# Zero fills between the single transfers of w_up, w_gate and their gradients in the FFN

## Chip, cores, metric

The kernel runs on one core of one Trainium2 chip. The metric is device time in microseconds (us) from launch to end; a kernel's executions agree within about 0.2%. A profiled execution has a span about 2 us shorter than the time that is quoted.

## The reference, cut to what matters

A decode step of one token is run forwards and backwards: adaptive layer norm, attention over the last 4096 positions of a 65536-long cache, a gated FFN. The outputs are the result and the gradients of every input.

```python
def _B_ref(x, w_gate, w_up, w_down):          # D = 1024, F = 3584
    g = jnp.einsum('bsd,df->bsf', x, w_gate)
    u = jnp.einsum('bsd,df->bsf', x, w_up)
    h = _sigmoid(g) * u
    return jnp.einsum('bsf,fd->bsd', h, w_down)
# attention, layer norms, modulation: left out
_out, _vjp = jax.vjp(_f, A_x, A_k_cache, A_v_cache, A_wq, A_wo, B_w_gate, B_w_up, B_w_down, c, w_mod)
```

Two things follow. The gradients of the two caches are zero outside the last 4096 positions, so 120 blocks of some 1 MB must be filled with zeros: 126 of the 186 MB written. They depend on nothing and can be issued at any moment. And with one token the weights are used once, so the kernel moves bytes far more than it computes.

## The kernel before

The FFN goes through F in 14 blocks of 256 columns. Loads of w_up and w_gate and the stores of their gradients are half a megabyte each and use the same three slots in turn; they go through GpSimd's queue, as do the fills. w_down and its gradient go through SyncE's. A row of a w_up block is 256 bf16 values, so its DRAM side is cut in runs of 512 bytes ("short runs" below).

```python
def zero(n, after=None):                 # issue the next n zero fills, 1 MB each
    for _ in range(n):
        if len(zleft) <= keep[0]:        # ten are kept for the end
            return
        ...                              # nc.gpsimd.dma_start(out=region, in_=zeros)

def load_ug(n):
    nc.gpsimd.dma_start(out=ug_slot[n % 3][:, 0, :, :], in_=wu_view[:, :, n * FB:(n + 1) * FB])
    nc.gpsimd.dma_start(out=ug_slot[n % 3][:, 1, :, :], in_=wg_view[:, :, n * FB:(n + 1) * FB])

for n in range(NB):
    ...                                  # gradients of block n into ug (VectorE, ScalarE)
    nc.sync.dma_start(out=wd_dram(out_8, n), in_=wd)        # w_down gradient
    ...                                  # load w_down of block n + 2; front(n + 1)
    nc.gpsimd.dma_start(out=dwu_view[:, :, n * FB:(n + 1) * FB], in_=ug[:, 0, :, :])
    st = nc.gpsimd.dma_start(out=dwg_view[:, :, n * FB:(n + 1) * FB], in_=ug[:, 1, :, :])
    zero(Z_FFN[2 * n])
    if n + 3 < NB:
        load_ug(n + 3)                   # waits until the two stores above have landed
    zero(Z_FFN[2 * n + 1])
```

A GpSimd issue that waits holds up all that stand behind it in the program.

## Time and profile before

| | before |
|---|---|
| time, median | 627.65 us (627.56 to 627.77, 3 runs) |
| bytes moved | 256.42 MB, mean 410 GB/s |
| busiest compute engine | VectorE, 52% of the span |
| rate, FFN (172 to 376 us) | 402 GB/s |
| rate, fills alone (155 to 160 us) | 429 GB/s |

A kernel whose DMA engines are busy in every slice gains only if it moves fewer bytes or moves them faster. So rates by stage are the first thing to read. A bare busy digit does not help: it is 9 in the FFN as well.

### The profile page before, as it was taken

Reading aid. Unit: us, or ns where it says so; the run is one execution under the profiler, and the core shown is the slowest. Engines: PE = TensorE matmul, PEld = TensorE weight load, DVE = VectorE, ACT = ScalarE, POOL = GpSimd, SP = SyncE. Lnnn points to the kernel's source line nnn. Section 1 sums busy time; section 2 is a strip of 40 time slices with the busy share of each in tenths; the row PEclk is TensorE's granted clock in tenths of the full one; section 3 lists DMA queues with packets and bytes.
Section 4 is the critical chain, followed back from the end, with each engine's and each line's share of the span. In section 5 each row is a group of like instructions: output and inputs, shape, how many; then the busy total and the mean of one; then the engine's idle time right before and its main releaser. Section 6 shows DMA issues by size and latency. Waiting matters only on the chain.

```text
span 625.3 us, 8430 instructions
## 1 busy us (share of the span) xinstructions
PE 188.0 (30%) x3324; PEld 164.8 (26%) x3324; DVE 325.4 (52%) x728; ACT 212.8 (34%) x333; POOL 151.4 (24%) x232
## 2 busy tenths in 40 slices
PE   3888176623022121111111113312920013225100
PEld 3877155622021121111111112210720012225000
DVE  3442046203986784746565456999740089930400
ACT  2652157100035342424333234984520013225300
POOL 2000121113223232324323342322311014312320
PEclk9876578655555555555555555555755555555555
DMA  9999999999999999999999999999999999999997
GB/s 353 421 423 418 422 418 420 424 424 423 422 386 389 404 394 407 407 401 409 411 401 407 399 405 417 415 420 426 423 426 424 423 421 429 425 428 426 426 422 263
DMA packets 42647, 256.42 MB, mean 410 GB/s; under 512 B 5149, under 2 KB 5149, under 8 KB 18080
## 3 DMA queue, kind: packets, MB, share of 16 engines
q0 software_dynamic: 31568, 192.95, 80.8%
q1 hardware_dynamic: 10992, 62.93, 29.4%
q8 instruction: 26, 0.43, 0.3%
q14 instruction: 13, 0.11, 0.0%
q10 hardware_dynamic: 48, 0.01, 0.0%
HBM read 70.26 MB, written 185.60 MB: 409 GB/s over the span
## 4 chain that ended last, share of the span: by engine, by line
DMA 65%; DVE 10%; PE 9%; issue 5%; ACT 5%; POOL 3%; ACTq 0%; POOLq 0%; DVEq 0%
DMA out_dram<-arena 34%; DMA out_dram<-zeros 12%; DVE arena L206 7%; DMA arena<-in_B_w_gate_dram 6%; DMA arena<-in_A_k_cache_dram 4%; DMA arena<-in_w_mod_dram 4%; DMA arena<-in_A_wo_dram 4%; PE tp_kv L440 2%; ACT arena L443 1%; POOL arena L539 1%; PE tm_w L349 1%; POOL out_dram L656 1%; ACT arena L824 1%; DMA rows<-in_c_dram 1%; ACT arena L237 1%
## 5 line engine op out<-in xcount | busy, mean ns | idle before, releaser
L171 POOL DMA_DIRECT2D out_dram<-zeros x114 | 64.2, 567 | 187.2 <-DMA out_dram<-zeros 55.2
L237 ACT ACTIVATE arena<-dug_b,h 128x512 bf16<-128x512 bf16 x112 | 71.4, 713 | 13.2 <-DVE dh2acc L206 12.1
L206 DVE CUSTOM_DVE_ANT_0 arena<-arena,dug_b 128x512 bf16<-128x512 bf16 x112 | 69.6, 686 | 0.5
L206 DVE CUSTOM_DVE_ANT_0 arena<-arena 128x1024 bf16<-128x1024 bf16 (+1 forms) x16 | 45.1, 2819 | 43.9 <-DMA arena<-in_w_mod_dram 39.0
L612 PE MATMUL gu_ps<-h_bf,arena 128*128 128x1 bf16 x448 | 16.0, 166 | 128.9 <-issue 97.9
L820 PEld LDWEIGHTS <-arena 8*128 8x128 bf16 x256 | 25.8, 131 | 101.1 <-issue 97.5
L612 PEld LDWEIGHTS <-arena 128*128 128x128 bf16 x448 | 14.1, 105 | 131.0 <-issue 98.4
L206 DVE CUSTOM_DVE_ANT_0 junk<-arena,b1k 128x1024 fp8e4<-128x1024 bf16 x28 | 34.2, 1223 | 15.9 <-DMA arena<-in_B_w_down_dram 15.4
L206 DVE CUSTOM_DVE_ANT_0 arena<-arena,b1k 128x1024 bf16<-128x1024 bf16 x32 | 37.2, 1219 | 0.0
L538 POOL DMA_DIRECT2D arena<-in_B_w_up_dram x14 | 12.8, 915 | 97.7 <-DMA out_dram<-arena 79.1
L824 ACT CAST arena<-ps_kv 128x512 bf16<-128x512 f32 x32 | 16.1, 692 | 57.1 <-DMA out_dram<-arena 57.1
L614 ACT ACTIVATE sg<-gu_ps 128x2 f32<-128x2 f32 x14 | 2.4, 171 | 93.8 <-PE gu_ps L612 93.8
L820 PE MATMUL ps_kv<-DO_hd,arena 8*128 8x128 bf16 x128 | 15.9, 296 | 57.2 <-ACT arena L824 57.2
L237 ACT ACTIVATE arena<-b1k,o_sh 128x1024 bf16<-128x1024 bf16 x24 | 27.2, 1152 | 11.1 <-DVE do_sh L206 11.1
L826 ACT ACTIVATE arena<-ps_kv 128x512 bf16<-128x512 f32 x32 | 16.1, 625 | 37.9 <-DMA out_dram<-arena 37.9
L440 PE MATMUL tp_kv<-ident_bf,arena 128*128 128x128 bf16 x256 | 22.2, 253 | 21.6 <-DMA arena<-in_A_k_cache_dram 13.8
L198 DVE COPY arena<-tp_kv 128x1024 bf16<-128x1024 bf16 x19 | 13.0, 691 | 29.1 <-PE tp_kv L440 29.0
L820 PE MATMUL ps_kv<-Q_hd,arena 8*128 8x128 bf16 x128 | 16.1, 295 | 37.9 <-ACT arena L826 37.9
L349 PEld LDWEIGHTS <-arena 128*128 128x128 bf16 x320 | 25.9, 124 | 0.0
L440 PEld LDWEIGHTS <-arena 128*128 128x128 bf16 x256 | 19.4, 115 | 24.4 <-DMA arena<-in_A_k_cache_dram 14.7
L636 PE MATMUL bc_ps<-ident_bf,dug_bf 128*128 128x128 bf16 x56 | 14.5, 475 | 33.5 <-DVE hh L189 33.5
L443 ACT COPY arena<-tp_kv 128x1024 bf16<-128x1024 bf16 x13 | 13.1, 1011 | 31.8 <-PE tp_kv L440 31.8
(228 smaller groups left out, 491.6 us busy)
## 6 DMA issues: line engine op xcount, KB each, us to landing
out_dram<-zeros POOLq DMA_DIRECT2D x114, 1024.0 KB, 17.2
out_dram<-arena POOLq DMA_DIRECT2D x32, 1024.0 KB, 19.1
out_dram<-arena POOLq DMA_DIRECT2D x36, 512.0 KB, 13.0
arena<-in_A_wq_dram SPq DMA_DIRECT2D x16, 1024.0 KB, 14.4
arena<-in_w_mod_dram SPq DMA_DIRECT2D x8, 1536.0 KB, 20.7
arena<-in_A_wo_dram SPq DMA_DIRECT2D x8, 1024.0 KB, 39.6
arena<-in_B_w_down_dram SPq DMA_DIRECT2D x14, 512.0 KB, 10.5
arena<-in_B_w_up_dram POOLq DMA_DIRECT2D x14, 512.0 KB, 11.5
```

The source lines that it names most:

```text
L171: ins = nc.gpsimd.dma_start(out=region.bitcast(FP32), in_=zeros[:, :])
L198: return nc.vector.tensor_copy(out=out, in_=a)
L206: return nc.vector.tensor_tensor_reduce(out=out, in0=w, in1=b, scale=1.0, scalar=0.0, op0=ALU.mult, op1=ALU.add, accum_out=acc)
L237: return nc.scalar.activation(out=out, in_=b, func=ACT.Copy, scale=col)
L349: nc.tensor.transpose(tp[:, nb * P:(nb + 1) * P], wm_t[j][:, c0:c0 + P], ident_bf[:, :])
L440: nc.tensor.transpose(tp[:, t8 * P:(t8 + 1) * P], src[:, g, t_ * DH:(t_ + 1) * DH], ident_bf[:, :])
L443: last = nc.scalar.copy(out=o, in_=tp[:, :])
L612: nc.tensor.matmul(gu[:, col + jj:col + jj + 1], lhsT=ug[:, k, j, jj::2], rhs=h2_bf[:, j:j + 1], start=(j == 0), stop=(j == KD - 1))
L636: nc.tensor.matmul(ps4[:, k // 2, :, k % 2], lhsT=r["dug_bf"][:, k:k + 1].broadcast_to([P, P]), rhs=ident_bf[:, :], start=(k == 0), stop=( ...
L820: nc.tensor.matmul(ps[:, t4 * DH:(t4 + 1) * DH], lhsT=rows[32 * g:32 * g + HG, t_ * P:(t_ + 1) * P], rhs=hd[32 * g:32 * g + HG, :], start= ...
L824: nc.scalar.copy(out=o, in_=ps[:, :])
L826: nc.scalar.activation(out=o, in_=ps[:, :], func=ACT.Copy, scale=float(scale))
```

## The change

Its intent: no long row of half-megabyte transfers with short runs; a fill stands between them wherever it can. The new lists also have more fills in the FFN (5 + 56 instead of 4 + 50; the later lists then run out earlier).

```diff
-Z_UG = [2, 0, 2]
-Z_FFN = [3, 0, 2, 1, 3, 0, 2, 1, 3, 0, 2, 0, 3, 0, 3, 1, 2, 2, 2, 1, 2, 4, 0, 3, 1, 5, 3, 1]
+Z_UG = [1, 1, 0, 1, 1, 1]
+Z_FFN = [1, 2, 1, 0, ... the same four numbers for each of the 14 blocks ...]
-    def load_ug(n):
-        nc.gpsimd.dma_start(... w_up ...)
-        nc.gpsimd.dma_start(... w_gate ...)
+    def load_ug(n, nz):
+        for k, view in ((0, wu_view), (1, wg_view)):
+            nc.gpsimd.dma_start(out=ug_slot[n % 3][:, k, :, :], in_=view[:, :, n * FB:(n + 1) * FB])
+            zero(nz[k])
     for n in range(3):
-        load_ug(n)
-        zero(Z_UG[n])
+        load_ug(n, Z_UG[2 * n:2 * n + 2])
...
         nc.gpsimd.dma_start(out=dwu_view[...], in_=ug[:, 0, :, :])
-        st = nc.gpsimd.dma_start(out=dwg_view[...], in_=ug[:, 1, :, :])
-        zero(Z_FFN[2 * n])
+        zero(Z_FFN[4 * n])
+        nc.gpsimd.dma_start(out=dwg_view[...], in_=ug[:, 1, :, :])
+        zero(Z_FFN[4 * n + 1])
         if n + 3 < NB:
-            load_ug(n + 3)
-        zero(Z_FFN[2 * n + 1])
+            load_ug(n + 3, Z_FFN[4 * n + 2:4 * n + 4])
+        else:
+            zero(Z_FFN[4 * n + 2] + Z_FFN[4 * n + 3])
```

More of the change, by code (lines that the diff above doesn't have):

```diff
@@ L50 @@
 Z_LN = 2
-Z_UG = [2, 0, 2]
-Z_FFN = [3, 0, 2, 1, 3, 0, 2, 1, 3, 0, 2, 0, 3, 0, 3, 1, 2, 2, 2, 1, 2, 4, 0, 3, 1, 5, 3, 1]
+Z_UG = [1, 1, 0, 1, 1, 1]
+Z_FFN = [1, 2, 1, 0, 1, 2, 1, 0, 1, 2, 1, 0, 1, 2, 1, 0, 1, 2, 1, 0, 1, 2, 1, 0, 1, 2, 1, 0, 1, 2, 1, 0, 1, 2, 1, 0, 1, 2, 1, 0, 1, 2, 1, 0, 1, 2, 1, 0, 1, 2, 1, 0, 1, 2, 1, 0]
 Z_END = [4, 0, 0, 0, 2, 0, 0, 0, 4]
@@ L535, in load_wd @@
         return nc.sync.dma_start(out=wd_slot[n % 2], in_=wd_dram(B_w_down, n))
-    def load_ug(n):
-        nc.gpsimd.dma_start(out=ug_slot[n % 3][:, 0, :, :], in_=wu_view[:, :, n * FB:(n + 1) * FB])
-        nc.gpsimd.dma_start(out=ug_slot[n % 3][:, 1, :, :], in_=wg_view[:, :, n * FB:(n + 1) * FB])
+    def load_ug(n, nz):
+        for k, view in ((0, wu_view), (1, wg_view)):
+            nc.gpsimd.dma_start(out=ug_slot[n % 3][:, k, :, :], in_=view[:, :, n * FB:(n + 1) * FB])
+            zero(nz[k])
     attn_ps = new_acc("attn_ps")
@@ L656 @@
         nc.gpsimd.dma_start(out=dwu_view[:, :, n * FB:(n + 1) * FB], in_=ug[:, 0, :, :])
-        st = nc.gpsimd.dma_start(out=dwg_view[:, :, n * FB:(n + 1) * FB], in_=ug[:, 1, :, :])
-        zero(Z_FFN[2 * n])
+        zero(Z_FFN[4 * n])
+        nc.gpsimd.dma_start(out=dwg_view[:, :, n * FB:(n + 1) * FB], in_=ug[:, 1, :, :])
+        zero(Z_FFN[4 * n + 1])
         if n + 3 < NB:
-            load_ug(n + 3)
-        zero(Z_FFN[2 * n + 1])
+            load_ug(n + 3, Z_FFN[4 * n + 2:4 * n + 4])
+        else:
+            zero(Z_FFN[4 * n + 2] + Z_FFN[4 * n + 3])
     ffn = vt([P, KD], "ffn")
```

## The prediction

> **What bounds the kernel now.** I read the page's slices first, then the stages by windows, then GpSimd's timeline in the FFN (its queue issues every transfer that the change moves), then VectorE's timeline near the end, for slack.
>
> ```profile
> DMA  9999999999999999999999999999999999999997
> GB/s 353 421 423 418 422 418 420 424 424 423 422 386 389 404 394 407 407 401 409 411 401 407 399 405 417 415 420 426 423 426 424 423 421 429 425 428 426 426 422 263
> DMA 65%; DVE 10%; PE 9%; issue 5%; ACT 5%; POOL 3%; ACTq 0%; POOLq 0%; DVEq 0%
> ```
>
> The 16 DMA engines have work in every slice; no compute engine is above 52% of the span. So time is bytes over rate: 256.42 MB at a mean of 410 GB/s. The rate is 420 to 429 nearly everywhere, and 386 to 411 in slices 12 to 24, which are the FFN. Windows of that stage (the last two numbers of a row are DMA share and GB/s):
>
> ```profile
> 155.00:160.00 5.00, 0.00 (x0) 0.00 (x0) 4.86 (x8) 0.00 (x0) 0.53 (x1) 0.50 1.15 429
> 185.00:190.00 5.00, 1.18 (x32) 1.01 (x32) 5.00 (x15) 2.58 (x7) 0.00 (x0) 0.50 1.05 334
> 172.00:376.00 204.00, 37.22 (x736) 33.81 (x735) 129.25 (x385) 78.45 (x149) 69.20 (x93) 0.50 1.14 402
> ```
>
> The first row is zero fills alone: 429. The second is nearly only w_up and w_gate loads, four of which were issued one behind another (168.4 to 177.4 us): 334. The third is the whole stretch: 402. GpSimd in one block of the FFN:
>
> ```profile
> 294.13 0.91 POOL L538 DMA_DIRECT2D arena<-in_B_w_up_dram  x1 [6.14 <-DMA out_dram<-arena]
> 295.56 1.04 POOL L539 DMA_DIRECT2D arena<-in_B_w_gate_dram  x1 [0.52 <-PE ffn_ps L641]
> 296.59 0.89 POOL L656 DMA_DIRECT2D out_dram<-arena  x1
> 297.48 0.89 POOL L657 DMA_DIRECT2D out_dram<-arena  x1
> 298.36 1.24 POOL L171 DMA_DIRECT2D out_dram<-zeros  x2
> 301.35 0.53 POOL L171 DMA_DIRECT2D out_dram<-zeros  x1 [1.75 <-DMA out_dram<-zeros]
> 309.54 0.91 POOL L538 DMA_DIRECT2D arena<-in_B_w_up_dram  x1 [7.66 <-DMA out_dram<-arena]
> ```
>
> Four half-megabyte transfers in a row, then the zero fills, then a wait until the w_up gradient has landed and freed its slot. A later zero fill waits for an older transfer to land: a zero fill takes 17.2 us from issue to landing, and one is done each 2.45 us, so some 7 or 8 are under way at most. That is the store of work that keeps the DMA engines busy while GpSimd waits. Last, VectorE in the final loop:
>
> ```profile
> 462.65 1.29 DVE L202 TENSOR_SCALAR arena<-arena,h 128x4096 bf16<-128x4096 bf16 x1
> 502.93 1.23 DVE L206 CUSTOM_DVE_ANT_0 arena<-arena 128x1024 bf16<-128x1024 bf16 x1 [38.99 <-DMA arena<-in_w_mod_dram]
> 505.40 4.42 DVE L206 CUSTOM_DVE_ANT_0 arena<-arena 128x4096 bf16<-128x4096 bf16 x1
> 513.52 4.42 DVE L206 CUSTOM_DVE_ANT_0 arena<-arena 128x4096 bf16<-128x4096 bf16 x1
> ```
>
> It sits idle for 39 us before the loop, so compute can come later without cost; within the loop a pass takes 513.52 - 505.40 = 8.1 us.
>
> **What the Trainium skill says.** "DMA: Bandwidth & Descriptors", section "Issuing engines are not separate DMA queues": all transfers run on the same 16 DMA engines and interleave, whoever issued them. The trace agrees: rates with and without the second queue active stay near 425. The same page, "Why small descriptors are slow (HBM only)", gives a fixed overhead of some 3 cycles per descriptor on 32-byte beats. Rows of w_up and w_gate blocks are 256 bf16 = 512 bytes, 16 beats, so the estimate from that page is 16/19 = 84% of its 435 GB/s ceiling, 366; for an 8 KB run 256/259, 430. The trace agrees roughly: 334 to 376 where these transfers dominate a window, 429 for zero fills. The point that decides: such a cost belongs to each descriptor, and an order doesn't remove it.
>
> **The change part by part.** (1) Order. In a block before: gradient, gradient, two or three zeros, load, load, zero or none. After: gradient, Z, gradient, Z Z, load, Z, load. The bytes are the same. At 428 GB/s the 82.0 MB of the stretch 172:376 (402 x 204) would take 191.6 us instead of 204: the whole excess is 12.4 us, 2.0% of the run. That is the ceiling of any gain from order. How much is order and how much is the short run? I counted the trace's packets by queue and size in steps of 2 us over this stretch and fitted a fixed time per packet of each kind. The fit gives 344 GB/s for these loads, 374 for these gradients, 429 for zeros, 419 for the w_down traffic, and leaves a residual of 0.08 us per 2 us step. The 6400 short-run packets of 4 KB are 26.2 MB and take 73.5 us by that fit, against 61.2 us at 428: 12.2 us. So an additive cost already explains the 12.4 us. Order shows only in what's left: windows with 20 to 40% of their bytes in short runs moved at 405 to 409, where the additive sum at 30% is about 402; windows nearly pure in short runs fell to 348 to 360. Short runs are about 30% of the stage's bytes; if all of it ran as the mixed windows do, 402 becomes 406, 1% of 204 us: 2 us gained.
>
> (2) Number and place of zero fills. The lists sum to 4 + 50 before and 5 + 56 after; of the 120 fills in all, ten are kept for the end both times, so the 7 more are taken from the last loop, which has 13 now and will have 6. The byte sum is equal. Before the last w_gate load stand 4 + 33 = 37 of them now, 5 + 44 = 49 after: that load lands 12 x 2.45 = 29 us later, and with it the FFN's end. After it, up to the end of the wo gradients, there are 28 now and 12 + 1 + 10 = 23 after, 5 fewer, 12 us given back. So the loop's start moves from 503 to about 520 us, and the loop then needs 7 x 2.45 = 17 us less. Sum: zero at the end.
>
> (3) Issue cost. Some 7 more fills of 0.57 us on GpSimd in the FFN: GpSimd is 34% busy there (69.2 of 204). Nothing.
>
> Sum: -2 us from order, 0 from moving fills, and about +0.5 us for small losses in the loop (below): 627.65 - 1.5, rounded to 626.
>
> **The rivals.** A: order matters much more, if short-run transfers hurt each other where they meet, in a way the additive fit does not see. For it: 334 GB/s at 185:190, the one place where four of these loads stand together. Against: the fit's residuals are small, and few windows are so pure. It would give 5 to 9 us: 619 to 622.
> B: the moved fills starve the engines later. Passes 2 to 7 of the last loop have 3.15 MB each (dwq, dk or dv, w_mod gradient), 7.4 us at 426 GB/s, while VectorE takes 8.1 us. Six passes without a filler lose 6 x 0.7 = 4.4 us of stored work. Seven to ten us are stored as the loop begins, and three fills follow at its first step, so I expect no gap; if I've misjudged the store, 2 to 6 us are lost: 628 to 632. For it: nothing fills behind 530 us. Against: the kernel before runs its last three passes without fills at 426.
> C: a zero fill between gradient and load delays the load, and the FFN waits on slots. ScalarE waits 93.8 us in total for the next block's gate matmuls, so loads do arrive just in time. But when GpSimd stops for the w_gate slot, Z Z load Z are still queued, 3.7 MB or some 9 us, and it needs no more than the landing of a gradient that is next in line; the FFN can't run the engines dry. It would be 1 us a block, 14 us, to reach 640; unlikely.
>
> **Range and chances.** 626.0 us, 8 in 10 between 621.5 and 629.5: the low end is half of rival A, the high end a mild B. Faster by over 2% needs below 615, all of the 12.4 us ceiling: 0.02. Slower by over 2% needs C: 0.02. Within 2%: 0.96.
>
> **What would show it.** In the windows of the changed kernel the FFN's rate should be 403 to 410, with fewer windows under 370; a mean of 415 or more would be rival A. The FFN's last gate matmuls should come near 400 us instead of 372, VectorE's wait for w_mod shrink from 39 us to some 27 and end near 518, and the last loop stay at 420 GB/s or more with DMA at 9 in all slices. A slice below 410 after 530 us would be B; FFN windows with DMA share below 0.9 would be C. If the rate rises in the FFN and the time doesn't fall, look for where it was lost in the loop.

## The result, and the profile after

The changed kernel takes 624.12 us (623.99 to 624.64, 4 runs) against 627.71 us (627.56 to 627.78, 4 runs). The ratio is 0.9945, 95% interval 0.9927 to 0.9962. The gain is 3.5 us, 0.55%: small but clear of noise, and within 2%.

The slices of the changed kernel:

```profile
DMA  9999999999999999999999999999999999999997
GB/s 351 422 421 421 421 418 420 423 425 423 423 403 408 408 410 410 411 411 408 411 411 409 411 412 409 413 419 414 427 426 421 423 424 419 428 426 425 423 424 273
```

The dips of the FFN are gone: 403 to 413 in slices 12 to 26, instead of 386 to 411 in 12 to 24. Outside, most slices moved by a few GB/s; the largest falls are in slice 28 (426 to 414) and slice 34 (429 to 419). Three windows of it follow, the first two being those shown of before at 334 and 402 GB/s. A row has the stretch and its length in us, the busy us of TensorE's matmuls and weight loads, VectorE, ScalarE and GpSimd (with the number of instructions), the granted clock, the DMA share and GB/s:

```profile
185.00:190.00 5.00, 2.52 (x52) 2.27 (x52) 3.94 (x12) 2.89 (x5) 0.00 (x0) 0.50 1.12 401
172.00:376.00 204.00, 32.05 (x632) 29.05 (x631) 118.73 (x348) 69.45 (x131) 67.54 (x93) 0.50 1.16 409
550.00:600.00 50.00, 17.20 (x185) 13.99 (x183) 24.33 (x43) 19.43 (x33) 16.65 (x25) 0.50 1.05 425
```

402 became 409, but not all of that is gain: the stretch now holds more fills and fewer short-run bytes, which alone raises its mean. GpSimd in one block of the FFN of the changed kernel (start, duration, line, what it issued, and in brackets the wait ahead of it with what ended it):

```profile
294.83 1.03 POOL L540 DMA_DIRECT2D arena<-in_B_w_up_dram  x1 [8.63 <-PE bc_ps L637]
295.85 0.54 POOL L171 DMA_DIRECT2D out_dram<-zeros  x1
299.56 0.91 POOL L540 DMA_DIRECT2D arena<-in_B_w_gate_dram  x1 [3.16 <-issue]
300.57 0.90 POOL L657 DMA_DIRECT2D out_dram<-arena  x1
301.46 0.56 POOL L171 DMA_DIRECT2D out_dram<-zeros  x1
302.01 0.90 POOL L659 DMA_DIRECT2D out_dram<-arena  x1
302.90 0.57 POOL L171 DMA_DIRECT2D out_dram<-zeros  x1
```

The order is the one wanted, and one pair is still close: the w_gate load and the next w_up gradient. The waits ahead of the loads (8.63 and 3.16 us) did not become shorter: from 140 to 400 us they sum to 129 us, before to 116. They cost nothing that shows, since no 5 us window between 170 and 400 us is under 385 GB/s. Last, the FFN's final gate matmuls, before and then after, and VectorE's wait ahead of the last loop, after:

```profile
372.38 0.59 PE L612 MATMUL gu_ps<-h_bf,arena 128*128 128x1 bf16 x16 [0.86 <-DMA arena<-in_B_w_gate_dram]
```

```profile
399.88 0.58 PE L613 MATMUL gu_ps<-h_bf,arena 128*128 128x1 bf16 x16 [3.70 <-DMA arena<-in_B_w_gate_dram]
...
518.01 1.23 DVE L206 CUSTOM_DVE_ANT_0 arena<-arena 128x1024 bf16<-128x1024 bf16 x1 [29.92 <-DMA arena<-in_w_mod_dram]
```

The FFN ends 27.5 us later and the program still ends earlier: moved fills are a shift of work, not a cost. Two waits of VectorE absorbed most of it: the one ahead of the last loop fell from 39.0 to 29.9 us, the one behind the loop from 25.1 to 7.8.

**A cost that can be compared.** To be free of the mix I took from the trace's packet records (a packet is one piece that a DMA engine moves) the stretch from the first to the last packet of the 56 short-run transfers (29.4 MB) and subtracted the fills in it (with some 0.2 MB of other queues) at 429 GB/s and the w_down traffic at 419. What is left I call the cost of the short-run transfers: 81.9 us before, 79.0 after. It also holds any time in which the queue ran dry. By kind, a packet (4 KB) of a w_up load took 183 ns before and 174 after, of a w_gate load 188 and 176; of the gradients 178 and 173 before, 176 and 175 after. So the loads became cheaper and the stores hardly did.

**From the transfers to the end of the program.** The cost fell by 2.9 us and the profiled span by 3.2 us (625.3 to 622.2), but these are not the same microseconds. At the end SyncE checks that all transfers have landed (its first check that passes marks the last landing), and GpSimd runs a DRAIN instruction that began with its last issue. Before and after (number; least, median and greatest duration in ns; first and last start in us):

```profile
L904 SPq EVENT_SEMAPHORE  x11: 17/28/28, 621.7 to 625.3; - x11
L904 POOLq DRAIN  x3: 46/102/17387, 607.2 to 625.1; - x3
```

```profile
L907 SPq EVENT_SEMAPHORE  x11: 17/28/28, 619.6 to 622.1; - x11
L907 POOLq DRAIN  x3: 46/102/16287, 605.1 to 621.9; - x3
```

The last transfer landed 2.1 us earlier (621.7 to 619.6). The other 1.1 us is GpSimd's DRAIN, which took 17.39 us before and 16.29 after and outlasted the last landing both times: the program ends 3.6 us behind that landing before, 2.5 after. So about a third of the gain is not faster transfers, and why the DRAIN became shorter stays open. And 2.1 is less than 2.9, mostly because the DMA engines finish less evenly after the change: the last 12 MB of packets took 30.3 us before and 31.0 after. From 596 us on, in slices of 0.75 us, before and after:

```profile
DMA  9999999999999999999999999999987420000000
```

```profile
DMA  9999999999999999999999998666620000000000
```

### The profile page after: what moved, and what is told of

It reads as the page before. It is cut to its first block, busy times and chain, and to the rows that moved or that the text cites. A ratio compares the mean times of both kernels' runs of the same rounds, so it can differ in the third digit from the quotient of the medians.

```text
span 622.2 us, 8426 instructions
## 1 busy us (share of the span) xinstructions
PE 186.5 (30%) x3324; PEld 163.6 (26%) x3324; DVE 326.3 (52%) x728; ACT 212.5 (34%) x333; POOL 148.2 (24%) x232
## 3 DMA queue, kind: packets, MB, share of 16 engines
q1 hardware_dynamic: 10992, 62.93, 29.9%
## 4 chain that ended last, share of the span: by engine, by line
DMA 59%; DVE 12%; issue 11%; PE 8%; POOL 4%; ACT 3%; ACTq 0%; POOLq 0%; SPq 0%; DVEq 0%
DMA out_dram<-arena 28%; DMA out_dram<-zeros 11%; DVE arena L206 7%; DMA arena<-in_w_mod_dram 6%; DMA arena<-in_B_w_gate_dram 5%; DMA arena<-in_A_k_cache_dram 4%; DMA arena<-in_B_w_down_dram 3%; PE tp_kv L440 2%; ACT arena L443 1%; PE tm_w L349 1%; DVE arena L202 1%; POOL out_dram L657 1%; POOL arena L540 1%; POOL out_dram L171 1%; PE tp_w L349 1%
## 5 line engine op out<-in xcount | busy, mean ns | idle before, releaser
L237 ACT ACTIVATE arena<-dug_b,h 128x512 bf16<-128x512 bf16 x112 | 71.4, 713 | 13.3 <-DVE dh2acc L206 13.3
L206 DVE CUSTOM_DVE_ANT_0 arena<-arena 128x1024 bf16<-128x1024 bf16 (+1 forms) x16 | 45.1, 2819 | 32.3 <-DMA arena<-in_w_mod_dram 29.9
L189 DVE TENSOR_TENSOR dug<-dhh,sg 128x2 f32<-128x2 f32 x14 | 2.3, 161 | 53.5 <-ACT sg L615 52.9
## 6 DMA issues: line engine op xcount, KB each, us to landing
out_dram<-arena POOLq DMA_DIRECT2D x36, 512.0 KB, 13.3
```

The lines of the kernel that those rows point to most:

```text
L206: return nc.vector.tensor_tensor_reduce(out=out, in0=w, in1=b, scale=1.0, scalar=0.0, op0=ALU.mult, op1=ALU.add, accum_out=acc)
L237: return nc.scalar.activation(out=out, in_=b, func=ACT.Copy, scale=col)
```

## The experiments

Theories at the start. Order: a fill between two short-run transfers makes them cheaper. Count: it is the seven more fills in the FFN, or the even four per block. All kernels have one more edit, because the check before the chip refuses an fp8 output of this VectorE form. The scratch tile is bf16 and shares its memory with two constants, which are written anew after the FFN:

```diff
-    junk = vt([P, D], "junk", FP8)
+    junk = shared            # bf16; ident_f and ones_f are views of it
+    nc.vector.memset(ones_f, 1.0)      # after the FFN
+    cp(ident_f, ident_bf)
```

In the table G is a gradient store, L a load (w_up, then w_gate), Z a fill, for one block. "Cost" is the cost just defined, "ns" the mean packet time of the w_up and w_gate loads, "landed" when SyncE saw the last landing in the profiled execution, "beside" the share of bytes belonging to loads among the packets that start within 0.3 us of one of theirs (again w_up, w_gate).

| run | block | time, us | ratio (95%) | cost, us | landed, us | ns | beside |
|---|---|---|---|---|---|---|---|
| before | GG ZZZ LL (3.57 Z on average) | 627.7 | 1 | 81.9 | 621.7 | 183, 188 | 0.56, 0.65 |
| the change | GZG ZZ LZL | 624.12 | 0.9945 (0.9927 to 0.9962) | 79.0 | 619.6 | 174, 176 | 0.32, 0.41 |
| after_again | the same | 623.98 | 0.9947 (0.9934 to 0.9959) | 78.9 | 619.6 | 174, 176 | as above |
| order_only | old numbers, GZGZLZL | 627.02 | 0.9988 (0.9976 to 1.0001) | 81.2 | 621.3 | 180, 178 | 0.42, 0.56 |
| count_only | GG ZZZ LL Z | 625.61 | 0.9972 (0.9959 to 0.9986) | 79.9 | 620.8 | 180, 182 | 0.40, 0.50 |
| all_apart | GZGZLZLZ | 625.04 | 0.9960 (0.9948 to 0.9973) | 79.8 | 620.1 | 176, 187 | 0.35, 0.35 |
| loads_apart | GG ZZZ LZL | 624.39 | 0.9954 (0.9941 to 0.9966) | 79.1 | 620.0 | 173, 176 | 0.32, 0.41 |
| grads_apart | GZG ZZ LL Z | 626.75 | 0.9991 (0.9979 to 1.0004) | 81.4 | 621.8 | 183, 190 | 0.53, 0.56 |
| two_between | GZGZ L ZZ L | 624.15 | 0.9953 (0.9940 to 0.9965) | 79.4 | 619.7 | 177, 176 | 0.34, 0.43 |
| old_count_at_loads | old numbers, GG ZZ LZL | 626.87 | 0.9991 (0.9978 to 1.0005) | 81.3 | 621.2 | 180, 179 | 0.46, 0.59 |

Cost, landings and times rank the runs nearly alike. The times also hold the DRAIN, so a difference of some 1 us is safer read from cost and landing: the program ended 3.6 us behind the last landing in before, order_only and old_count_at_loads, 2.9 in count_only, all_apart and grads_apart, and 2.5 in the others. Each landing is that of one profiled execution; the change and its control after_again agree (619.6). Where the interval of the ratio reaches 1 (order_only, grads_apart, old_count_at_loads), a gain in time is not clear of noise.

### Control

> Control: the changed kernel with its scratch tile moved (bf16 in place of fp8; the check asks for it), so two tiny extra VectorE operations after the FFN. Every theory: the same 3.5 us under the kernel before as the changed kernel, 623.7 to 624.6 us, FFN rate between 172 and 376 us at 408 to 410 GB/s. If it differs by over 0.5 us, the scratch tile is not neutral and the other runs must be read against this one alone.

623.98 us: the scratch tile is neutral.

### Order or count

```diff
 # order_only: the change's code, the old numbers in each block
-Z_UG = [1, 1, 0, 1, 1, 1]
+Z_UG = [1, 1, 0, 0, 1, 1]
+Z_FFN = [1, 1, 1, 0] (blocks of 3), [1, 0, 1, 0] (of 2), [1, 2, 1, 0] (of 4), ...
 # count_only: the old code, the new numbers
-Z_UG = [2, 0, 2]
+Z_UG = [2, 1, 2]
+Z_FFN = [3, 1] * 14
```

> The number of zero fills in each block of the FFN as before (50 in the blocks, 4 at the first loads), only their place as in the change. Theory order (short-run transfers cost less when a fill runs beside them): nearly the whole gain stays, 2.5 to 3.5 us under before. Theory count (7 more fills in the FFN dilute the short runs, or the even number per block is what helps): under 1 us of gain.

> The number of zero fills as in the change (4 a block, 5 at the first loads), their places as before: three behind the two gradients, one behind the two loads. Theory order: under 1 us of gain. Theory count: 2.5 to 3.5 us of gain.

Measured: 0.7 and 1.8 us by the ratios; by the landings 0.4 and 0.9. Neither theory holds as I put it; order alone is a miss for mine. Two readings help. First, the order did work where a block has enough fills. These are the rates of before, then of order_only, then of the change:

```profile
172.00:300.00 128.00, 24.25 (x476) 21.93 (x475) 87.31 (x258) 52.24 (x98) 44.00 (x58) 0.50 1.15 400
300.00:376.00 76.00, 12.97 (x260) 11.88 (x260) 41.93 (x128) 26.22 (x51) 25.20 (x35) 0.50 1.11 404
```

```profile
172.00:300.00 128.00, 23.95 (x476) 21.74 (x475) 88.03 (x258) 51.90 (x98) 41.54 (x55) 0.50 1.12 399
300.00:376.00 76.00, 11.52 (x240) 10.51 (x240) 40.67 (x123) 24.01 (x48) 27.16 (x39) 0.50 1.15 409
```

```profile
172.00:300.00 128.00, 21.67 (x424) 19.54 (x423) 78.96 (x230) 46.20 (x87) 39.92 (x55) 0.50 1.16 409
300.00:376.00 76.00, 10.38 (x208) 9.50 (x208) 39.77 (x119) 23.25 (x44) 27.62 (x39) 0.50 1.15 410
```

From 300 us on order_only is as fast as the change (409 and 410, before 404), with the old numbers. Free of the mix, by the same subtraction in this stretch, 4 KB of short runs cost 176 ns there (in 16 engines' time), 175 in the change and 181 before. Up to 300 us it gains nothing (185 ns, as before). There it has one place where the queue ran dry, in the block with two fills:

```profile
280.00:285.00 5.00, 0.75 (x18) 0.66 (x16) 4.43 (x13) 4.01 (x7) 1.45 (x2) 0.50 0.93 302
```

```profile
270.50 0.56 POOL L172 DMA_DIRECT2D out_dram<-zeros  x1
271.06 0.90 POOL L660 DMA_DIRECT2D out_dram<-arena  x1
280.68 0.89 POOL L541 DMA_DIRECT2D arena<-in_B_w_up_dram  x1 [8.72 <-PE ffn_ps L643]
```

A DMA share under 1 and 302 GB/s: in the 8.7 us in which GpSimd waited to issue the load at 280.68, the queue held only one fill and one gradient behind the w_up gradient that it waited for. Those 5 us lose 1.3 us against 409 GB/s. The other place is the first loads, where w_gate of block 1 and w_up of block 2 are still neighbours (212 and 198 ns a packet; 189 and 187 in the change). So I read it that the number matters by what it does in thin blocks; no run fills only those.

Second, in count_only the fill behind the two loads keeps them from the next gradients but not from each other.

### All apart

```diff
-Z_FFN = [1, 2, 1, 0] * 14
+Z_FFN = [1, 1, 1, 1] * 14
```

> As the change, but the two fills behind the w_gate gradient are split: one stays, one goes behind the w_gate load, so that no two short-run transfers are neighbours at all. Theory order: the pair load w_gate and next gradient w_up also comes apart, a quarter of the neighbour pairs, so 0.5 to 1 us better than the change, some 623.3 us. Theory count: the same as the change.

625.04 us, 1 us worse than the change: a second miss. The most even order is not the best. The w_up loads cost 176 ns, but the w_gate loads 187, as before. What they have beside them differs in one thing: the w_down gradient, which comes through the other queue, is 10% of the bytes beside a w_gate load in the change and 3% here (3% in grads_apart too, where a packet takes 190). That the w_down gradient is what the w_gate load misses is argued from these records, not shown by a run, and two records speak against it: beside the w_gate loads of count_only and the w_up loads of two_between it has 4%, and their packets take 182 and 177 ns.

### Loads or gradients

The new theory: the loads pay for running beside other loads; stores do not care.

```diff
-Z_FFN = [1, 2, 1, 0] * 14
+Z_FFN = [0, 3, 1, 0] * 14      # loads_apart
+Z_FFN = [1, 2, 0, 1] * 14      # grads_apart, with Z_UG = [0, 2, 0, 1, 0, 2]
```

> Four fills a block as in the change, but the two gradients stay neighbours: gradient, gradient, three fills, load, fill, load. New theory loads (the short-run loads are what costs extra, and only where no writes run beside them; gradients do not care): most of the change's gain stays, 2.3 to 3.5 us under before, mean packet time of the loads about 175 ns as in the change (185 before). Theory gradients or both: 1 to 2 us, like the run with the count alone (1.8).

> Four fills a block, between the gradients and not between the loads: gradient, fill, gradient, two fills, load, load, fill. Theory loads: no more than the count alone gave, 1 to 2 us under before, loads at 180 ns or more. Theory gradients: 2.5 to 3.5 us.

2.9 us and 0.6 us; by the landings 1.7 us earlier than before and 0.1 later. With the gradients side by side again nearly all of the gain stays; with the loads side by side nearly none does. The packet times say the same: 173 and 176 ns against 183 and 190. This pair settles which transfers matter: the loads, and the fill between the two. Three things it leaves open. count_only has the loads side by side too and still gained; what differs is one fill, which stands ahead of the loads there and between the gradients in grads_apart, and grads_apart has one slow place that costs about 1 us (321 GB/s from 210 to 215 us). And "beside" does not decide alone: with 0.56 the w_gate packets took 178 ns in order_only, with 0.55 190 in grads_apart. And no run tells whether the neighbour has to be a write or only a transfer with long runs.

### Runs of 4 KB

The same bytes are read and written in the same transfers and order, but the four arrays are cut into 4 KB runs instead of 512-byte rows.

```diff
+    def run4k(t):
+        return t.rearrange("d f -> (d f)").rearrange("(n p j f) -> n p j f", n=NB, p=P, j=KD)
+    wg_view, wu_view, dwg_view, dwu_view = (run4k(t) for t in (B_w_gate, B_w_up, out_6, out_7))
```

> Wrong result on purpose: the kernel before (scratch tile moved), with w_up, w_gate and their gradients read and written as blocks of 4 KB runs in DRAM instead of 512-byte rows. Same bytes, transfers, waits and order. Prediction's claim (the whole deficit of the FFN is the short run): 10 to 13 us under before, some 615 to 617 us, FFN rate 420 GB/s or more. Rival (the deficit comes from half-megabyte transfers that change direction and queue, whatever the run): under 4 us.

> Wrong result on purpose: the changed kernel with 4 KB runs. If only short runs care for their neighbours: within 1 us of the kernel before with 4 KB runs. If any load gains from writes beside it: 1.5 to 3.5 us better than that one.

long_before takes 620.64 us, ratio 0.9895 (0.9882 to 0.9909): 6.6 us gained, not 10 to 13. Its last transfer landed 9.1 us earlier (612.6); the program ended 5.5 us behind that, where it was 3.6. long_after takes 620.07 us, 0.9884 (0.9869 to 0.9899), and landed at 612.8. Their outputs are wrong, which doesn't matter for the times. Their FFN windows:

```profile
172.00:376.00 204.00, 37.75 (x738) 34.27 (x737) 136.12 (x414) 83.64 (x157) 52.18 (x97) 0.50 1.13 418
```

```profile
172.00:376.00 204.00, 32.30 (x648) 29.38 (x647) 118.15 (x349) 69.47 (x131) 49.98 (x93) 0.50 1.15 422
```

The run length is the largest single part, but not the whole. By the cost of the transfers: 81.9 us becomes 73.5 with long runs; at 428 GB/s it would be 68.6. With long runs the change's places and numbers still save 1.7 us of cost (73.5 to 71.8), but about 1 us of it is one place of long_before where the queue ran dry:

```profile
344.00:347.00 3.00, 0.00 (x0) 0.00 (x0) 0.00 (x0) 0.00 (x0) 2.58 (x5) 0.50 0.82 279
```

The packets of the loads fall only from 163 and 165 ns to 162 and 160, with short runs from 183 and 188 to 174 and 176. The times are 0.6 us apart with ratios whose intervals overlap: the branch "within 1 us" of the expectation, that only short runs care. That long runs do not care at all is not shown. None of the 1.7 us reached the landing, since the last 12 MB took 31.1 us in long_after and 29.5 in long_before. What the last 3 us above 68.6 are stays open.

### The loads on the other queue

If the loads need writes beside them, a queue of their own would give them that always.

```diff
-            nc.gpsimd.dma_start(out=ug_slot[n % 3][:, k, :, :], in_=view[...])
+            nc.sync.dma_start(out=ug_slot[n % 3][:, k, :, :], in_=view[...])
```

> Places and numbers of the fills as before; only the w_up and w_gate loads are issued by SyncE, on the second queue, so that they always run beside what GpSimd's queue holds, which is nearly only writes (fills and gradients). Theory loads-beside-writes: the loads no longer depend on where the fills stand in GpSimd's order, so 2.5 to 5 us under before without the change's order. Theory order in one queue (what helps is the fill between two transfers of the same queue): 0 to 1 us. A loss would mean that SyncE's in-order waits (for the gradient to land before the next load) hold up the w_down traffic.

> The changed kernel with the loads on SyncE's queue. Theory loads-beside-writes: within 1 us of the run above (order of the fills no longer matters), and about as good as or up to 2 us better than the change. Theory order in one queue: the change's gain stays, about 3.5 us, and is clearly better than the run above.

657.52 us and 654.70 us, ratios 1.0486 (1.0472 to 1.0501) and 1.0438 (1.0424 to 1.0453): the loss that the expectation named last, and far larger than I thought. sp_before in the FFN:

```profile
280.00:285.00 5.00, 0.58 (x16) 0.50 (x16) 0.00 (x0) 2.51 (x6) 0.00 (x0) 0.50 0.41 122
```

```profile
300.12 1.64 POOL L172 DMA_DIRECT2D out_dram<-zeros  x3
318.73 0.91 POOL L657 DMA_DIRECT2D out_dram<-arena  x1 [16.98 <-ACT arena L238]
```

The DMA engines stand idle much of the time (share 0.41). In SyncE's program the loads wait for the gradients to land, and the w_down traffic stands behind them: from 268.5 to 283.1 us SyncE issues nothing. The blocks' compute then comes late, VectorE waits 72 us in total for w_down between 200 and 400 us, and GpSimd waits for gradients (17 us here) with nothing else to issue. A second candidate is not separated from this: on SyncE's queue the records show the loads as 28672 packets of 512 bytes, 31 ns each, so 4 KB take 250 ns there, against some 186 ns for a 4 KB packet on GpSimd's queue before. So these runs say nothing of the neighbours; the theory they were to test was not reached.

### Two fills between the loads

```diff
-Z_FFN = [1, 2, 1, 0] * 14
+Z_FFN = [1, 1, 2, 0] * 14
```

> Four fills a block: gradient, fill, gradient, fill, load, two fills, load. As many neighbours of the loads are fills as in the change, and the loads are further apart. Theory loads-beside-writes: within 1 us of the change, 623 to 625 us; if the w_gate load then no longer runs beside the w_down gradient, its packets rise to 180 ns or more and the time to 625.

624.15 us, as good as loads_apart and not better than the change; the w_gate packets stay at 176 ns. One fill between the loads is enough.

### The old numbers, all at the loads

```diff
+Z_UG = [1, 1, 0, 0, 1, 1]
+Z_FFN = [0, 2, 1, 0] (blocks of 3), [0, 1, 1, 0] (of 2), [0, 3, 1, 0] (of 4), ...
```

> The numbers of fills per block exactly as before (50 in the blocks, 4 at the first loads), none between the gradients: all ahead of the w_up load and one between the loads. If what matters is only the fills ahead of and between the loads, the older number suffices: 2 to 3 us under before, loads at 174 to 179 ns. If the even and larger number per block is needed as well (order alone with the old numbers gave 0.7): 0 to 1.2 us, and then a part of the change's gain belongs to the number.

0.6 us (0.5 by the landings): the low branch of the expectation. Place alone does not do it with the old numbers. As in order_only the rate is 399 up to 300 us and 409 after it, so again it is the early blocks of two or three fills that pay nothing. The share of loads beside loads stays at 0.46 and 0.59: with fewer fills the loads still meet each other.

No order tried beats the change.

## Why the prediction was right or wrong

It said 626.0 us, 621.5 to 629.5, within 2%; 624.12 came. That the number is so close is in part luck: 1.1 us of the 3.2 us in the span is GpSimd's DRAIN, of which the prediction knew nothing, and the 2 us that it gave to order alone came from order and number together.

- *The bound is bytes over rate*: right up to the last landing, which came 2.1 us earlier: 2.9 us of cost saved in the FFN, about 0.7 lost again over the last 12 MB, though the FFN's end moved by 27.5 us. The shorter DRAIN behind the landing is not part of this bound.
- *The moved fills cancel*: right. Predicted were the last gate matmuls near 400 us (399.9), VectorE's wait of some 27 us ending near 518 (29.9, 518.0), the last loop at 420 or more (423 from 500 to 550 us, 425 from 550 to 600).
- *FFN at 403 to 410 and fewer windows under 370*: right; 409, and of the 5 us windows between 170 and 400 us none is below 385, where before four were below 370.
- *"An additive cost already explains the 12.4 us"*: this step was wrong. The fit gave each kind one price, so whatever the loads paid for being neighbours went into that price. With 4 KB runs 6.6 us come back in time, 9.1 at the last landing, 8.4 in the transfers' cost, out of 13.3 (81.9 less 68.6). The deficit has a part that is not run length.
- *"2 us gained" from order*: 2.9 us in the transfers, but order alone at the old numbers gave 0.7 of it (81.9 to 81.2) and the new numbers at the old places 2.0 (to 79.9). It also spread the gain over all short runs, whereas the loads have nearly all of it.
- *The number of fills is worth zero*: wrong as a claim on the FFN. It cancels as a matter of bytes, but the old numbers leave thin blocks in which the order cannot work: with them the new places gave 0.7 and 0.6 us, neither clear of noise.
- *"+0.5 us for small losses in the loop"* (a mild rival B): the size is about right, the place is not. The loop's rate is at most 2 GB/s lower, which in 100 us is under 0.5 us; the uneven end costs about 0.7.
- *Rival A* ("in a way the additive fit does not see"): its mechanism fits, for loads. Its size, 5 to 9 us, does not. *Rival C*: not seen in the change; waits of this kind show in the runs with loads on SyncE's queue.

On the Trainium skill: the estimate of 366 GB/s for 512-byte runs from "DMA: Bandwidth & Descriptors", section "Why small descriptors are slow (HBM only)", lies between the 358 (29.4 MB in 81.9 us) and 372 GB/s (in 79.0 us) that these transfers had before and after. But the section puts this overhead on packets and says that joined descriptors share it, and the records of GpSimd's queue show packets of 4 KB for these rows; for a packet of 4 KB the same estimate gives 425. (The section's second cost, metadata for every descriptor, the prediction left out.) So the agreement of the value does not show the cause. And "the point that decides", that an order does not remove the cost, failed: the transfers' descriptors stayed the same and their cost fell from 81.9 to 79.0 us.

## What to carry to other kernels

In this kernel, and perhaps in others whose DMA engines are always busy: look for stretches where short-run loads have nothing but loads beside them, and put a store that can go at any time between them; between stores it gives little. Give every block enough of such fillers: the one thin block of order_only in which the queue ran dry lost 1.3 us, more than the 0.7 us that this run gained in all. A price per packet fitted over one kernel's trace mixes what a transfer costs with what its neighbours cost, so test it by changing the run length or the order alone. And before a gain of a few us is put down to transfers, compare the last landings: what follows them changed by 1.1 us here and by up to 1.8 in the experiments.

## What the Trainium skill lacked or had wrong

- "DMA: Bandwidth & Descriptors", section "Why small descriptors are slow (HBM only)": it gives fixed costs per packet and per descriptor and nothing of neighbours. Here the same descriptors cost 81.9 to 79.0 us by order and number of fills, and a load's packet took 173 to 190 ns, while those of the gradients kept within 170 to 179.
- The same section: for 4 KB runs the estimate by its rule is 128/131 of 435, 425 GB/s. Half-megabyte transfers with such runs had 400 (29.4 MB in 73.5 us) and 409 GB/s (in 71.8 us).
- The same page, section "Rules for kernel authors": it says that spreading transfers over issuing engines doesn't help and only saves issue time, not that it can cost. Moving the loads to SyncE cost some 30 us here (657.5 against 627.2 us before, 654.7 against 624.1 of the change).
- No page that I read has it: GpSimd's closing DRAIN outlasts the last landing, and the program ended 2.5 to 5.5 us behind that landing in kernels that differ only in the order, number, runs or queue of their transfers.
